# One program order for all engines from a list-scheduled model; transposes of the first two batches on TensorE

## The chip, the cores and the metric

The kernel runs on one core of one Trainium2 chip. The metric is the device time of one execution in microseconds. A profiled execution gives a trace: each engine's instructions with start and length, the DMA queues, and the clock that TensorE was granted. Engines are named as in the profile: PE is TensorE's matmul side, PEld its weight loads, DVE is VectorE, ACT is ScalarE, POOL is GpSimd, SP is SyncE; an added q (SPq) means the engine's queue of instructions that it issues, such as DMAs.

## The reference

For 8 batches, 12 heads, 448 positions and head size 64, q and k are normalized by their root mean square over the head dimension and multiplied by a gain vector each; then softmax attention; then the heads are put side by side (3584 tokens of 768) and go through a feed-forward layer with a gate.

```python
q_n, k_n = rmsnorm(q, g_q), rmsnorm(k, g_k)        # x / sqrt(mean(x*x) + 1e-6) * g
attn = softmax(q_n @ k_n.T / sqrt(64))
x = (attn @ v)  -> (3584, 768)
h = x @ w_in                                       # 768 x 2048
out = (h * sigmoid(1.702 * h)) @ w_out             # 2048 x 768, float32
```

## The kernel before

Work goes by pairs of heads: 48 pairs, numbered i, six to a batch. A sequence of 448 is 4 blocks of 112. Per pair the steps are these.

- `load`: three DMAs from SP bring q, k and v of the pair (112 partitions, 224 KB each), into a ring of 7 pairs.
- `square` (POOL, line 166) and `reduce` (DVE, line 173) give sums of squares. `rsqrt` (DVE, lines 187 to 198) makes the inverse root for a group of pairs: pairs 0, 1 and 2 are groups of one, the others go by threes. It is a bit trick and two Newton steps, 11 small operations on 16 (one pair) or 48 (three pairs) elements.
- `norm` (POOL, line 206, one operation for q and one for k) writes the normalized tile `qkn` in bf16; `vcast` (DVE, line 214) writes v in bf16 to `vx`.
- `dmaT` (line 219): one DMA transpose from SP turns `qkn` to `qT`. `pad` (DVE, line 228) scales k by the gains into `kz`, twice (one half of the partitions each).
- `Sc`: per block of 112 keys two matmuls to a score tile `sc` (PSUM, two buffers), and one `exp` on ACT (line 240) to `att`.
- `PV`: per head 16 matmuls of 65 columns to `o`, then a reciprocal and a multiply on DVE (lines 259, 260) to `obs`.
- `OT` (line 272): one DMA transpose from SP puts the pair's 128 rows into `xT[b]`.

When the six pairs of a batch are in `xT[b]`, its feed-forward can run: 16 tiles `gp` of 6 matmuls (line 299), a tanh on ACT (line 307) and a gate on DVE (line 309) for each, then the second product `op`, 16 matmuls a tile (line 327), a copy on ACT (line 334) and a store from SP. The weights come by DMAs from POOL's queue with a cast to bf16 (lines 378 and 388).

The order of every engine's instructions is the order in which the program emits them. It is written by hand: a loop over pairs emits a block of scores, PV of the pair before at blocks 0 and 2, the steps for later pairs (`ahead`: loads 7 pairs ahead, squares 6, reduces 5, norms 2), and then `fill` puts in feed-forward matmuls worth 1525 ns of a small clock that the emission keeps. That clock delays the emission of evictions, gates, transposes and pads by fixed times (`later`). At the start `start` emits seven pairs of loads (21 DMAs), then the steps of pair 0, the six loads of `w_in`, squares up to pair 5, and the four loads of `w_out`. The program ends with all the feed-forward that is left.

Of the kernel before, what the change touches and what calls it, by code (L numbers as in the profile page):

```python
# [18 lines left out]
_MAGIC = 0x5F3759DF  # L19


@with_exitstack
def kernel(
# [24 lines left out]
    AW = (NS - 1) * SS + WIN  # L48

# [56 lines left out]
    raw = [None] * NG  # L106
    vraw = [None] * NG
    rs = [None] * NG
    qkn = [None] * NG
    qT = [None] * NG  # L110
    obs = [None] * NG
    xT = [None] * B
    groups = [[0], [1], [2], [3, 4, 5]] + [list(range(j, j + 3)) for j in range(6, NG, 3)]
    group_of = {p: g for g in groups for p in g}
    ssq_of = {}

    clk = 0.0
    events = []  # L120
    seq = 0

    done = set()

    def later(dt, f, tag=None):
        nonlocal seq
        seq += 1
        heapq.heappush(events, (clk + dt, seq, f, tag))

    def step():  # L130
        nonlocal clk
        t, _, f, tag = heapq.heappop(events)
        clk = max(clk, t)
        f()
        done.add(tag)

    def tick(dt):
        nonlocal clk
        end = clk + dt
        while events and events[0][0] <= end:  # L140
            step()
        clk = end

    def need(*tags):

        while any(t not in done for t in tags):
            step()

    def load(i):
        b, h0 = i // NP, 2 * (i % NP)  # L150
        t = raw_p.tile([128, 2, 2, NS, D], FP32, tag="raw", name="raw")
        for gi, src in enumerate((q, k)):
            nc.sync.dma_start(  # L153
                out=t[:SS, gi, :, :, :],
                in_=src[b, h0:h0 + 2].rearrange("h (ss ns) d -> ss h ns d", ns=NS))
        tv = vraw_p.tile([128, 2, NS, D], FP32, tag="vraw", name="vraw")
        nc.sync.dma_start(
            out=tv[:SS, :, :, :],
            in_=v[b, h0:h0 + 2].rearrange("h (ss ns) d -> ss h ns d", ns=NS))
        raw[i], vraw[i] = t, tv  # L160

    sq_of = {}

    def square(i):
        sq = sq_p.tile([128, 2, 2, NS, D], FP32, tag="sq", name="sq")
        nc.gpsimd.tensor_tensor(out=sq[:SS], in0=raw[i][:SS], in1=raw[i][:SS], op=ALU.mult)  # L166
        sq_of[i] = sq

    def reduce(i):
        grp = group_of[i]  # L170
        if i == grp[0]:
            ssq_of[grp[0]] = stat_p.tile([128, 3, 2, 2, NS], FP32, tag="ssq", name="ssq")
        nc.vector.reduce_sum(out=ssq_of[grp[0]][:SS, i - grp[0]], in_=sq_of.pop(i)[:SS],  # L173
                             axis=AX.X)

    def rsqrt(i):
        grp = group_of[i]
        if i != grp[-1]:
            return

        m = len(grp) * 4 * NS
        x = ssq_of[grp[0]][:SS].rearrange("p a b c d -> p (a b c d)")[:, :m]
        y = stat_p.tile([128, 3, 2, 2, NS], FP32, tag="rs", name="rs")
        yf = y[:SS].rearrange("p a b c d -> p (a b c d)")[:, :m]
        t = small_p.tile([128, 3 * 4 * NS], FP32, tag="nt", name="nt")
        tf = t[:SS, :m]
        nc.vector.tensor_scalar(out=x, in0=x, scalar1=float(D) * 1e-6, scalar2=None,
                                op0=ALU.add)
        nc.vector.tensor_scalar(out=tf.bitcast(I32), in0=x.bitcast(I32), scalar1=1,  # L189
                                scalar2=None, op0=ALU.arith_shift_right)  # L190
        nc.vector.tensor_tensor(out=yf.bitcast(I32), in0=magic[:SS, :m],
                                in1=tf.bitcast(I32), op=ALU.subtract)
        for _ in range(2):
            nc.vector.tensor_tensor(out=tf, in0=yf, in1=yf, op=ALU.mult)  # L194
            nc.vector.tensor_tensor(out=tf, in0=tf, in1=x, op=ALU.mult)  # L195
            nc.vector.tensor_scalar(out=tf, in0=tf, scalar1=-0.5, scalar2=1.5,  # L196
                                    op0=ALU.mult, op1=ALU.add)
            nc.vector.tensor_tensor(out=yf, in0=yf, in1=tf, op=ALU.mult)  # L198
        for p in grp:
            rs[p] = (y, p - grp[0])  # L200

    def norm(i):
        y, a = rs[i]
        t = qkn_p.tile([128, 2, NS, 2, D], BF16, tag="qkn", name="qkn")
        for gi in range(2):
            nc.gpsimd.tensor_tensor(  # L206
                out=t[:SS, gi],
                in0=raw[i][:SS, gi].rearrange("p h n d -> p n h d"),
                in1=y[:SS, a, gi].rearrange("p h n -> p n h").to_broadcast([SS, NS, 2, D]),
                op=ALU.mult)  # L210
        qkn[i] = t

    def vcast(i):
        nc.vector.tensor_copy(out=vx_ring[i % N_V][:SS, :, :, :D], in_=vraw[i][:SS])  # L214

    def dmaT(i):

        t = qT_p.tile([128, 2, NS * SS], BF16, tag="qT", name="qT")
        nc.sync.dma_start_transpose(
            out=t[:, :, :].rearrange("p g (n s) -> p (g n) s", s=SS),  # L220
            in_=qkn[i][:SS].rearrange("s g n h d -> s (g n h d)"))
        qT[i] = t

    def pad(i):
        kz = kz_ring[i % N_KZ]
        for hp in range(2):
            r = slice(64 * hp, 64 * hp + 64)
            nc.vector.tensor_scalar(out=kz[r, hp, :], in0=qT[i][r, 1, :], scalar1=gG[r, :],  # L228
                                    scalar2=None, op0=ALU.mult)


    def Sc(i, kc):
        need(("T", i))
        sc = ps_sc.tile([128, 2, 512], FP32, tag="sc", name="sc")
        for hp in range(2):
# [3 lines left out]
            tick(190)  # L239
        later(250, lambda: nc.scalar.activation(  # L240
            out=att_ring[i % N_ATT][:SS, kc, :, :S], in_=sc[:SS, :, :S], func=ACT.Exp), ("E", i, kc))

    def PV(i, hp):
        need(*[("E", i, kc) for kc in range(NS)])
        att, vx = att_ring[i % N_ATT], vx_ring[i % N_V]
# [216 lines left out]
```

## Time and profile before

| | |
|---|---|
| median of 3 runs | 529.82 us (528.68 to 531.94) |
| the profiled execution | 535.25 us, of which span 533.5 us |
| mean granted TensorE clock | 0.958 |
| busy: PE, PEld | 441.6 us (83%), 270.6 us (51%) |
| busy: DVE, ACT, POOL | 311.8 (58%), 266.1 (50%), 199.5 us (37%) |

The busy share of TensorE in 40 equal slices of the span (13.3 us each; a digit is tenths), and the granted clock in tenths below it:

```profile
PE   0005175589999799999997999999999999999996
PEclk9999987559999899999998999999999999999999
```

Full clock is 2.4 GHz, the other level is 1.2 GHz. The time of an execution is 1.75 us longer than its span.

### The profile page before, as it was taken

What the parts mean: (1) busy time and instruction counts of PE and PEld (TensorE: products, weight loads), DVE (VectorE), ACT (ScalarE), POOL (GpSimd) and SP (SyncE); (2) the same over time, 40 slices, a digit from 0 to 9 for tenths busy, and PEclk for the clock granted to TensorE, in tenths of its full rate; (3) what the DMA queues carried; (4) which work ended last, traced back from release to release, by engine and by line L of the source; (5) the groups of instructions that cost most, each with busy time, mean ns of one, the idle gap of its engine ahead of it and who ended that gap; (6) DMA issues with size and microseconds to landing.
All of it is one profiled execution on the core that took longest, in us unless ns stands there. A gap on an engine that the chain in (4) does not pass through costs nothing.

```text
span 533.5 us, 9224 instructions
## 1 busy us (share of the span) xinstructions
PE 441.6 (83%) x3584; PEld 270.6 (51%) x3584; DVE 311.8 (58%) x719; ACT 266.1 (50%) x377; POOL 199.5 (37%) x165
## 2 busy tenths in 40 slices
PE   0005175589999799999997999999999999999996
PEld 0002043345665356665664566656665666565553
DVE  3254276766848684669487856487669564621500
ACT  0004053436656464576564655666576556752421
POOL 2773635543435343533526353535253440000000
PEclk9999987559999899999998999999999999999999
DMA  6999946473577535884679347747684433112012
GB/s 152 228 226 181 210 125 151 105 173 80 117 140 163 136 80 149 174 169 89 124 176 186 79 92 185 163 102 124 166 174 113 88 91 74 36 39 76 1 40 80
DMA packets 109964, 67.46 MB, mean 126 GB/s; under 512 B 71264, under 2 KB 105568, under 8 KB 109920
## 3 DMA queue, kind: packets, MB, share of 16 engines
q1 hardware_dynamic: 106944, 60.58, 52.0%
q0 software_dynamic: 2976, 6.29, 6.7%
q8 instruction: 28, 0.46, 0.4%
q14 instruction: 16, 0.13, 0.1%
HBM read 45.61 MB, written 11.01 MB: 106 GB/s over the span
## 4 chain that ended last, share of the span: by engine, by line
PE 62%; DMA 13%; DVE 12%; POOL 4%; SPq 3%; issue 3%; ACT 1%; POOLq 0%; DVEq 0%
PE op L327 25%; PE gp L299 22%; DMA qT<-qkn 9%; PE sc L236 9%; PE o L251 7%; DMA raw<-in_k_dram 4%; POOL sq L166 3%; DVE kz L228 3%; DVE ssq L173 2%; DVE g L309 2%; DVE obs L260 1%; POOL qkn L206 1%; SPq L153 1%; DVE nt L189 1%; DVE nt L195 1%
## 5 line engine op out<-in xcount | busy, mean ns | idle before, releaser
L240 ACT ACTIVATE att<-sc 112x896 bf16<-112x896 f32 x192 | 174.3, 916 | 179.1 <-PE sc L236 178.0
L236 PE MATMUL sc<-qT,kz 128*112 128x448 bf16 x384 | 117.1, 392 | 74.0 <-DVE kz L228 72.2
L299 PE MATMUL gp<-xt,w_in_s 128*128 128x448 bf16 x768 | 164.2, 359 | 10.1 <-DVE g L309 9.2
L166 POOL TENSOR_TENSOR sq<-raw 112x1024 f32<-112x1024 f32 x48 | 92.2, 1922 | 195.0 <-DMA raw<-in_k_dram 77.5
L327 PE MATMUL op<-w_out_s,g 128*128 128x384 bf16 x896 | 159.2, 326 | 0.0
L206 POOL TENSOR_TENSOR qkn<-raw,rs 112x512 bf16<-112x512 f32 x96 | 101.4, 1077 | 45.1 <-DVE rs L198 31.6
L327 PEld LDWEIGHTS <-g 128*128 128x128 bf16 x896 | 85.0, 98 | 54.3
L299 PEld LDWEIGHTS <-w_in_s 128*128 128x128 bf16 x768 | 73.6, 99 | 75.3 <-issue 15.8
L236 PEld LDWEIGHTS <-kz 128*112 128x112 bf16 x384 | 52.2, 141 | 107.2 <-DVE kz L228 82.2
L309 DVE SCALAR_TENSOR_TENSOR g<-th,gp 128x448 bf16<-128x448 f32 x128 | 78.0, 619 | 45.6 <-ACT th L307 44.2
L307 ACT ACTIVATE th<-gp 128x448 f32<-128x448 f32 x128 | 69.4, 542 | 44.9 <-PE gp L299 42.7
L228 DVE TENSOR_SCALAR kz<-qT,gG 64x448 bf16<-64x448 bf16 x96 | 59.0, 615 | 54.3 <-DMA qT<-qkn 53.3
L251 PEld LDWEIGHTS <-att 112*128 112x128 bf16 x1536 | 67.4, 103 | 20.8 <-DVE obs L260 5.6
L251 PE MATMUL o<-vx,att 112*128 112x65 bf16 x1536 | 70.7, 201 | 2.9 <-DVE obs L260 2.8
L173 DVE TENSOR_REDUCE ssq<-sq 112x16 f32<-112x1024 f32 x48 | 58.0, 1210 | 13.3 <-POOL sq L166 13.2
L259 DVE RECIPROCAL rcp<-o 112x4 f32<-112x4 f32 x96 | 17.3, 180 | 68.8 <-PE o L251 68.5
L334 ACT ACTIVATE osb<-op 128x384 f32<-128x384 f32 x56 | 27.4, 489 | 38.3 <-PE op L327 36.9
L260 DVE TENSOR_TENSOR obs<-o,rcp 112x256 bf16<-112x256 f32 x96 | 40.8, 425 | 3.3
L214 DVE CAST vx<-vraw 112x512 bf16<-112x512 f32 x48 | 22.8, 475 | 0.0
L194 DVE TENSOR_TENSOR nt<-rs 112x48 f32<-112x48 f32 (+1 forms) x36 | 9.0, 249 | 1.2
L195 DVE TENSOR_TENSOR nt<-nt,ssq 112x48 f32<-112x48 f32 (+1 forms) x36 | 8.9, 246 | 1.2
L196 DVE TENSOR_SCALAR nt<-nt 112x48 f32<-112x48 f32 (+1 forms) x36 | 8.3, 230 | 1.2
(18 smaller groups left out, 35.3 us busy)
## 6 DMA issues: line engine op xcount, KB each, us to landing
raw<-in_q_dram SPq DMA_DIRECT2D x48, 224.0 KB, 3.3
raw<-in_k_dram SPq DMA_DIRECT2D x48, 224.0 KB, 3.6
vraw<-in_v_dram SPq DMA_DIRECT2D x48, 224.0 KB, 4.0
w_in_s<-in_moe_w_in_dram POOLq DMA_DIRECT2D x6, 512.0 KB, 15.5
w_out_s<-in_moe_w_out_dram POOLq DMA_DIRECT2D x4, 768.0 KB, 20.5
out_dram<-osb SPq DMA_DIRECT2D x8, 336.0 KB, 3.2
out_dram<-osb SPq DMA_DIRECT2D x8, 288.0 KB, 3.0
out_dram<-osb SPq DMA_DIRECT2D x8, 240.0 KB, 3.0
```

What stands on the lines that cost most here:

```text
L166: nc.gpsimd.tensor_tensor(out=sq[:SS], in0=raw[i][:SS], in1=raw[i][:SS], op=ALU.mult)
L173: nc.vector.reduce_sum(out=ssq_of[grp[0]][:SS, i - grp[0]], in_=sq_of.pop(i)[:SS], axis=AX.X)
L206: nc.gpsimd.tensor_tensor(out=t[:SS, gi], in0=raw[i][:SS, gi].rearrange("p h n d -> p n h d"), in1=y[:SS, a, gi].rearrange("p h n -> p n h ...
L228: nc.vector.tensor_scalar(out=kz[r, hp, :], in0=qT[i][r, 1, :], scalar1=gG[r, :], scalar2=None, op0=ALU.mult)
L236: nc.tensor.matmul(sc[:SS, hp, :S], lhsT=kz_ring[i % N_KZ][:, hp, kc * SS:(kc + 1) * SS], rhs=qT[i][:, 0, :], start=True, stop=True)
L240: later(250, lambda: nc.scalar.activation(out=att_ring[i % N_ATT][:SS, kc, :, :S], in_=sc[:SS, :, :S], func=ACT.Exp), ("E", i, kc))
L251: nc.tensor.matmul(o[:, qs, :], lhsT=att[:SS, kc, hp, qs * SS:qs * SS + WIN], rhs=vx[:SS, hp, kc, :], start=(kc == 0), stop=(kc == NS - 1))
L260: nc.vector.tensor_tensor(out=obs[i][:SS, :, hp, :], in0=o[:SS, :, :D], in1=rcp[:SS, :].to_broadcast([SS, NS, D]), op=ALU.mult)
L299: nc.tensor.matmul(ps[:, :], lhsT=w_in_s[:, ki, m * 128:(m + 1) * 128], rhs=xT[b][:, ki, :], start=(ki == 0), stop=(ki == KI - 1))
L307: later(250, lambda: nc.scalar.activation(out=th[:, :], in_=ps[:, :], func=ACT.Tanh, scale=0.851))
L309: later(1000, lambda: nc.vector.scalar_tensor_tensor(out=g_of[b // 2][:, m, lo:lo + S], in0=th[:, :], scalar=1.0, in1=ps[:, :], op0=ALU.ad ...
L327: nc.tensor.matmul(ps[:, :], lhsT=g_of[b // 2][:, ko, tm * 128:(tm + 1) * 128], rhs=w_out_s[:, ko, half * HALF:(half + 1) * HALF], start=( ...
```

## The change

The hand-written emission goes away. Each instruction, or a few of one engine, is a task with an engine, an assumed duration in ns, a latency, a priority key, predecessors, and at times a slot of a ring that it takes. A list scheduler (`_Order.run`) plays the engines against a clock: an engine that is free takes the ready task with the lowest key, and the task's instructions are emitted at that moment. So the program order on each engine is the order of the model; on the chip the engines run it in order. The keys are in units of pairs: scores of pair i at i + block/4, feed-forward at 7.3 plus the work already listed over 5800 ns, steps that prepare pair i at i minus 1 to i minus 3.

What the instructions are changes too:

- squares run on ACT, in two halves for pairs 0 and 1;
- of the inverse root DVE keeps two operations (`seed`), and POOL does the other nine (`rsqrt`);
- `vcast` is on POOL, as a multiply by a column of ones;
- for pairs 0 to 11 `qkn` and `obs` are turned by TensorE (8 and 4 transposes of 112 x 128) into a PSUM buffer of the ring of three that the feed-forward uses, and DVE copies them out (`take_q`, `take_k`, `take_x`); the other 36 pairs keep the two DMA transposes;
- `pad` walks its elements in another order (112 groups of 4, step 112);
- `w_in` is loaded in four parts of 512 columns in place of six of 128 rows, from 13 us on by the model's clock, 6.5 us apart; `w_out` from 42 us on, 7 us apart;
- the four small loads of the gains and the load of pair 0's k are issued by ACT.

```diff
-    def square(i):
-        nc.gpsimd.tensor_tensor(out=sq[:SS], in0=raw[i][:SS], in1=raw[i][:SS], op=ALU.mult)
+    def square(i, part):
...
+        nc.scalar.activation(out=sq_of[i][:SS, part], in_=raw[i][:SS, part], func=ACT.Square)
...
+    def rsqrt(grp):
...
+        nc.gpsimd.tensor_tensor(out=yf.bitcast(I32), in0=magic[:SS, :m], in1=t.bitcast(I32),
+                                op=ALU.subtract)
         for _ in range(2):
-            nc.vector.tensor_tensor(out=tf, in0=yf, in1=yf, op=ALU.mult)
...
+            nc.gpsimd.tensor_tensor(out=t, in0=yf, in1=yf, op=ALU.mult)
...
     def vcast(i):
-        nc.vector.tensor_copy(out=vx_ring[i % N_V][:SS, :, :, :D], in_=vraw[i][:SS])
+        nc.gpsimd.tensor_tensor(out=vx[:, :, :D], in0=vr,
+                                in1=ones[:SS, :].to_broadcast([SS, 2 * NS, D]), op=ALU.mult)
+    def turn_pe(i):
+        tps[i] = ps_w.tile([128, 2, NS, SS], BF16, tag="w", name="t_ps")
...
+                nc.tensor.transpose(tps[i][:, gi, s, :], qkn[i][:SS, gi, s, :, :],
+                                    ident[:SS, :SS])
+    def take_q(i):
...
+        nc.vector.tensor_copy(out=qT[i][:, 0, :],
+                              in_=tps[i][:, 0].rearrange("p n s -> p (n s)"))
+    def take_k(i, hp):
+        nc.vector.tensor_scalar(out=kz_ring[i % N_KZ][r, hp, :],
+                                in0=tps[i][:, 1].rearrange("p n s -> p (n s)")[r],
+                                scalar1=gG[r, :], scalar2=None, op0=ALU.mult)
+    def pad(i, hp):
+            out=kz_ring[i % N_KZ][r, hp, :].rearrange("p (n s) -> p s n", s=SS),
+            in0=qT[i][r, 1, :].rearrange("p (n s) -> p s n", s=SS),
...
+        for j, part in enumerate(parts):
+            od.add(("S", i, j), "ACT", 920 / len(parts) + 80,
+                   lambda i=i, p=part: square(i, p), i - 3,
...
+            od.add(("Q", i), "POOL", 2300 if len(group_of[i]) > 1 else 1700,
+                   lambda g=group_of[i]: rsqrt(g), i - 2.6, deps=[("Q0", i)])
+        for gi in range(2):
+            od.add(("N", i, gi), "POOL", 1080, lambda i=i, gi=gi: norm(i, gi), i - 2.4,
+                   deps=[("Q", group_of[i][-1]), ("T", i - N_QKN)])
+        od.add(("V", i), "POOL", 1000, lambda i=i: vcast(i), i - 1.6,
+               deps=[("L", i, 2), ("P", i - N_V, 1, NS - 1)])
+        if i < ON_PE:
+            od.add(("T", i), "PE", 400, lambda i=i: turn_pe(i), i - 1.0,
...
+        else:
+            od.add(("T", i), "SP", 400, lambda i=i: turn_dma(i), i - 10.0,
...
+        for kc in range(NS):
+            od.add(("C", i, kc), "PE", 380, lambda i=i, kc=kc: score(i, kc), i + kc / 4,
+                   deps=[("K", i, 0), ("K", i, 1), ("KQ", i)], lat=250,
+                   takes=("sc", ("E", i, kc)))
+            od.add(("E", i, kc), "ACT", 917, lambda i=i, kc=kc: expo(i, kc), i + kc / 4 - 1,
+                   deps=[("C", i, kc), ("P", i - N_ATT, 1, NS - 1)])
...
+    for c in range(4):
+        od.add(("WI", c), "POOL", 800, lambda c=c: load_in(c), -50, at=13000.0 + 6500.0 * c,
...
+        od.add(("WO", c), "POOL", 800, lambda c=c: load_out(c), -50, at=42000.0 + 7000.0 * c,
...
+    PACE = 5800.0
+    for b in range(B):
+        for m in range(MI):
+            key = 7.3 + done / PACE
+            od.add(("F", b, m), "PE", KI * 189, lambda b=b, m=m: first(b, m), key,
+                   deps=[("X", b * NP + p) for p in range(NP)] + [("WI", m // 4), last],
+                   lat=250, takes=("w", ("G", b, m)))
+            done += KI * 189
...
+    od.run()
```

## Rows read from the trace of the kernel before

**Rows 1.** The page's first part: busy us (share of span) x instructions.

```profile
span 533.5 us, 9224 instructions
PE 441.6 (83%) x3584; PEld 270.6 (51%) x3584; DVE 311.8 (58%) x719; ACT 266.1 (50%) x377; POOL 199.5 (37%) x165
```

**Rows 2.** Windows: stretch, length, busy us (x count) per engine, clock, DMA, GB/s.

```profile
0.00:42.50 42.50, 0.00 (x0) 0.00 (x0) 17.11 (x51) 1.28 (x1) 24.87 (x33) 1.00 0.99 199
42.50:116.20 73.70, 40.78 (x306) 23.81 (x307) 42.94 (x94) 29.02 (x33) 34.02 (x26) 0.77 0.77 154
116.20:490.40 374.20, 362.63 (x3065) 225.50 (x3062) 241.79 (x559) 223.15 (x320) 140.58 (x107) 0.99 0.56 122
490.40:533.50 43.10, 38.17 (x219) 21.33 (x218) 9.94 (x16) 12.61 (x24) 0.00 (x0) 0.99 0.16 46
```

**Rows 3.** Waits up to 116.2: who, for whom, us, times, longest.

```profile
PE sc L236 <- DVE kz L228: 72.2, 15, 42.5
DVE kz L228 <- DMA qT<-qkn: 24.0, 6, 10.4
```

**Rows 4.** Timeline of the start: start us, us, engine, line, operation.

```profile
7.72 1.89 POOL L166 TENSOR_TENSOR sq<-raw 112x1024 f32<-112x1024 f32 x1 [6.35 <-DMA raw<-in_k_dram]
13.24 2.19 POOL L206 TENSOR_TENSOR qkn<-raw,rs 112x512 bf16<-112x512 f32 x2 [3.63 <-DVE rs L198]
15.37 3.40 POOL L378 DMA_DIRECT2D w_in_s<-in_moe_w_in_dram  x6
20.45 19.82 SPq L219 DMA_TRANSPOSE qT<-qkn  x2
```

**Rows 5.** Tile qT: the transposes' time from issue to landing.

```profile
DMA to landing us min/median/max: 2.9/4.1/21.6
```

**Rows 6.** Chain of waits at the start: start us, us, what.

```profile
3.92 3.65 DMA raw<-in_k_dram
```

**Rows 7.** Timeline around the first feed-forward matmul.

```profile
116.23 2.06 PE L299 MATMUL gp<-xt,w_in_s 128*128 128x448 bf16 x5
```

**Rows 8.** Groups by line and shape: count | busy us, mean ns | idle before.

```profile
L240 ACT ACTIVATE att<-sc 112x896 bf16<-112x896 f32 x192 | 174.3, 916 | 179.1 <-PE sc L236 178.0 <-ACT th L307 0.2
L307 ACT ACTIVATE th<-gp 128x448 f32<-128x448 f32 x128 | 69.4, 542 | 44.9 <-PE gp L299 42.7 <-DVE nt L189 0.7 <-DVE nt L196 0.6
L206 POOL TENSOR_TENSOR qkn<-raw,rs 112x512 bf16<-112x512 f32 x96 | 101.4, 1077 | 45.1 <-DVE rs L198 31.6 <-issue 13.5
L166 POOL TENSOR_TENSOR sq<-raw 112x1024 f32<-112x1024 f32 x48 | 92.2, 1922 | 195.0 <-DMA raw<-in_k_dram 77.5 <-DVE ssq L173 58.0 <-DVE vx L214 18.9
L214 DVE CAST vx<-vraw 112x512 bf16<-112x512 f32 x48 | 22.8, 475 | 0.0
L194 DVE TENSOR_TENSOR nt<-rs 112x16 f32<-112x16 f32 x6 | 1.0, 174 | 0.2
L173 DVE TENSOR_REDUCE ssq<-sq 112x16 f32<-112x1024 f32 x48 | 58.0, 1210 | 13.3 <-POOL sq L166 13.2
L309 DVE SCALAR_TENSOR_TENSOR g<-th,gp 128x448 bf16<-128x448 f32 x128 | 78.0, 619 | 45.6 <-ACT th L307 44.2
L260 DVE TENSOR_TENSOR obs<-o,rcp 112x256 bf16<-112x256 f32 x96 | 40.8, 425 | 3.3
L299 PE MATMUL gp<-xt,w_in_s 128*128 128x448 bf16 x768 | 164.2, 359 | 10.1 <-DVE g L309 9.2 <-DMA xt<-obs 0.7
L251 PE MATMUL o<-vx,att 112*128 112x65 bf16 x1536 | 70.7, 201 | 2.9 <-DVE obs L260 2.8
L240 ACT ACT_TABLE_LOAD x1 | 1.3, 1283 | 0.7 <-PEq L446 0.7
```

**Rows 9.** Tile kz: the pads' shortest, median and longest ns.

```profile
L228 DVE TENSOR_SCALAR kz<-qT,gG x96: 320/339/1962, 41.6 to 463.6; 64x448 bf16<-64x448 bf16 x96
```

**Rows 10.** The page's sixth part: weight loads, KB each, us from issue to landing.

```profile
w_in_s<-in_moe_w_in_dram POOLq DMA_DIRECT2D x6, 512.0 KB, 15.5
w_out_s<-in_moe_w_out_dram POOLq DMA_DIRECT2D x4, 768.0 KB, 20.5
```

More of the change, by code (lines that the diff above doesn't have):

```diff
@@ L137, in tick @@
[L137 to L149, printed above, removed]
-        b, h0 = i // NP, 2 * (i % NP)
[L151 to L160, printed above, removed]
@@ L199, in rsqrt, with norm @@
         for p in grp:
             rs[p] = (y, p - grp[0])
[L202 removed]
+    def norm(i, gi):
         y, a = rs[i]
[L204 to L211 removed]
@@ L238, in Sc, with expo @@
                              rhs=qT[i][:, 0, :], start=True, stop=True)
[L239 to L245, printed above, removed]
+    def expo(i, kc):
+        nc.scalar.activation(out=att_ring[i % N_ATT][:SS, kc, :, :S],
+                             in_=scs.pop((i, kc))[:SS, :, :S], func=ACT.Exp)
@@ new lines, with first, tanh @@
+    g_of, gps, ops = {}, {}, {}
+    def first(b, m):
+        ps = gps[b, m] = ps_w.tile([128, S], FP32, tag="w", name="gp")
+        for ki in range(KI):
+            nc.tensor.matmul(ps[:, :], lhsT=w_in_s[:, ki, m * 128:(m + 1) * 128],
+                             rhs=xT[b][:, ki, :], start=(ki == 0), stop=(ki == KI - 1))
+    ths = {}
+    def tanh(b, m):
+        th = ths[b, m] = th_p.tile([128, S], FP32, tag="th", name="th")
+        nc.scalar.activation(out=th[:, :], in_=gps[b, m][:, :], func=ACT.Tanh, scale=0.851)
@@ new lines, in gate, with second @@
+    def gate(b, m):
+        if m == 0 and b % 2 == 0:
+            g_of[b // 2] = g_p.tile([128, MI, 2 * S], BF16, tag="g", name="g")
+        lo = (b % 2) * S
+        nc.vector.scalar_tensor_tensor(
+            out=g_of[b // 2][:, m, lo:lo + S], in0=ths.pop((b, m))[:, :], scalar=1.0,
+            in1=gps.pop((b, m))[:, :], op0=ALU.add, op1=ALU.mult)
+    def second(bp, tm, hf, c):
+        if c == 0:
+            ops[bp, tm, hf] = ps_w.tile([128, HALF], FP32, tag="w", name="op")
+        for ko in range(4 * c, 4 * c + 4):
+            nc.tensor.matmul(ops[bp, tm, hf][:, :],
+                             lhsT=g_of[bp][:, ko, tm * 128:(tm + 1) * 128],
+                             rhs=w_out_s[:, ko, hf * HALF:(hf + 1) * HALF],
+                             start=(ko == 0), stop=(ko == MI - 1))
@@ L393, in ahead @@
-    def ahead(i, s):
-        if s == 0:
-            if i + LOAD < NG:
-                load(i + LOAD)
-            if i + SQ < NG:
-                square(i + SQ)
-        if s == 1 and i + RED < NG:
-            reduce(i + RED)
-        if s == 2 and i + RED < NG:
-            rsqrt(i + RED)
-        if s == 1 and i + NORM < NG:
-            prepare(i + NORM)
-    def prepare(j):
-        norm(j)
-        vcast(j)
-        later(2600, lambda: dmaT(j))
-        later(6000, lambda: pad(j), ("T", j))
@@ L413 @@
-    start()
-    tick(2000)
-    for i in range(NG + 1):
-        for s in range(NS):
-            if i < NG:
-                Sc(i, s)
-            if s == 0 and i > 0:
-                PV(i - 1, 0)
-            if s == 2 and i > 0:
-                PV(i - 1, 1)
-            ahead(i, s)
-            fill(per_gap)
-        if i > 0:
-            OT(i - 1)
-    while ready < B - 1:
-        step()
-    fill(1e12)
-    tick(1e9)
-    assert pos == len(moe)
+    PACE = 5800.0
+    done = 0.0
+    last = None
```

480 lines of the change are left out of this document (295 added, 185 removed).

## The prediction

> **What bounds the kernel now.** I read the page's busy shares first [rows 1]: TensorE is busy 441.6 of 533.5 us, the others half the span. So either TensorE's own work is the bound or its idle time is. The windows by stage answer that [rows 2]. Up to 42.5 us TensorE does nothing. From 42.5 to 116.2 us it is busy 40.78 of 73.70 us at a mean granted clock of 0.77, that is, partly at the lower of the two levels. From 116.2 us to the end it is busy 362.63 + 38.17 = 400.8 of 417.3 us at 0.99. At 116.23 us the first feed-forward matmul starts [rows 7]; it needs the rows of all six pairs of batch 0. So the kernel has two parts: a start of 116 us in which TensorE has only attention to do and waits 42.5 + 32.9 = 75.4 us, and 417 us in which it is the bound and waits 16.5 us. A faster engine helps the second part little; what the change can win lies in the first.
>
> Who ends the waits there [rows 3]: of TensorE's waits, 72.2 us end with the pad of k, and 24.0 us of the pad's own with the transposing DMA. The timeline shows how [rows 4]: the first pair's q and k are normalized at 13.24 + 2.19 = 15.43 us, but SyncE comes to their transpose at 20.45 us, behind 21 loads, and is held 19.82 us by the first two, among loads, weights and transposes that all use the DMA engines at a share near 1 [rows 2]. A transpose lands 4.1 us after its issue in the median and 21.6 us at worst [rows 5]. Squares of 1.92 us and norms of 2 x 1.08 us a pair [rows 8] stand in line on GpSimd besides, with the issue of the weight loads (3.40 us) between [rows 4].
>
> **The start after the change, in steps.** Data of pair 0: k was issued at 3.92 us behind four small loads and landed 3.65 us later, at 7.57 us [rows 6]. It now stands behind the same four on ScalarE's queue; I leave 7.57. Square of half a pair on ScalarE: the exp of 896 elements takes 916 ns and the tanh of 448 takes 542 [rows 8], so 0.835 ns an element and 168 ns fixed; 512 elements 0.60 us, 1024 elements 1.02 us. Half a reduce: 1.21/2 + 0.05 = 0.66 us. Two seed operations: 2 x 0.174 = 0.35 us.
>
> Newton on GpSimd is not in the trace. Its two-input operations there cost 1922 ns for 1024 elements and 1077 for 512, so 1.65 ns an element and some 0.23 us fixed: I take 0.25 us for 16 elements and 0.30 for 48, nine of them 2.25 and 2.7 us. Lower end: VectorE's 0.174 us; upper end: 0.5 us, half a norm. The value cast I take at a norm's 1.08 us, as it has the same shape and two inputs. The rows speak against moving these: the cast took 0.475 us on VectorE [rows 8]. The Trainium skill (GPSIMD Engine Reference, Engine selection) says likewise that elementwise work with two inputs runs about twice as slow there as on VectorE. By that factor alone, an estimate, a Newton operation would be 0.35 us, and the time below would come out some 3 us longer.
>
> So norms of pair 0 end at 7.57 + 0.60 + 0.66 + 0.35 + 2.25 + 2.15 = 13.6 us. From there GpSimd sets the pace, with 0.57 us for each weight part that it issues (3.40/6): cast and issue 1.65, Newton and norms 4.4 for pair 1: 19.7; the same for pair 2: 25.7; cast and issue: 27.4; Newton for the group 3 to 5: 30.1; three pairs of norms, two casts, one issue 9.2: 39.3 us. Then pair 5: eight transposes on TensorE, 1.0 us (bounds for one: 46 ns, as an o matmul in the stream, and 0.2 us, its length alone [rows 8]); three evictions by VectorE from PSUM, 0.6 us each (the gate's 619 ns for the same 448 elements is the nearest): 42.1; four exps and one square that gets between: 4 x 0.916 + 1.02 = 4.7: 46.8; last PV and its division 1.7: 48.5; four transposes and a copy 1.2: 49.7 us.
>
> TensorE may bind instead. At full clock a pair costs 8 x 0.214 + 70.7/48 = 3.2 us [rows 8], at half clock 6.4. Scores of pair 0 can start at 13.6 + 2.8 = 16.4 us; six pairs at half clock and the last steps of 1.8 us give 56.6 us. I take 52 us for the first feed-forward matmul, nearer the GpSimd end, since the clock was 0.77 in the stretch of this kind [rows 2]. VectorE has 1.3 + 0.35 + 1.8 + 2 x 0.6 + 0.6 = 5.3 us a pair, under GpSimd's 6.1. Low end 46 (Newton at 0.174, full clock), high end 60 (Newton at 0.5 us adds 36 x 0.23 = 8 us).
>
> **The rest.** 417.3 us stays [rows 2]. At 116.2 us TensorE had done 306 matmuls, 7.65 pairs of 40; at 52 us it will have done 6, so 1.65 x 3.2 = 5.3 us are still to do. The transposes of pairs 6 to 11 are 72 more, 3.3 to 14 us by the bounds above; I take 5.
>
> The other engines have room where TensorE goes by pairs: 40.35 pairs in 374.2 us, 9.3 us each. ScalarE then has 4 x 0.916 + 1.02 + 2.67 x 0.542 + 0.6 = 6.7 us; VectorE loses the cast and nine small operations; GpSimd changes squares (1.92) for cast and Newton (1.08 + 0.9). The pads have cost 320 ns free and up to 1962 [rows 9], the long ones beside a square of GpSimd; with another walk I give them 0.3 to 1.1 us and nothing on the path, because a pair's transposes may start as soon as the scores three pairs earlier are done, some 18 us ahead, against 4.1 us to land. If that cover goes, the price is a stall of TensorE per pair.
>
> The idle time of the second part, 16.5 us, I leave: a new fixed order may remove what waits for the gate (9.2 us, [rows 8]) and may add as much. Sum of the span: 52 + 417.3 + 5.3 + 5 = 479.6 us, and 1.75 us around it, 481.4 us against the profiled 535.25. The median of the runs is 0.990 of the profiled time (529.82/535.25), so **477 us**.
>
> **Rivals.** A: *the frozen order gives part of it back.* Engines run in order what a model with fixed durations has listed, and TensorE's place for a score group is where the model frees one of two score buffers. If score groups and gates come late by 0.1 to 0.15 us on average, some 300 places cost 30 to 45 us: 507 to 520 us. For it: no slack in the model at these places. Against it: the assumed durations (380 ns for two scores, 917 an exp, 1080 a norm) are those of the rows.
>
> B, the other side: *ScalarE's queue holds each score buffer.* Behind each of 168 score groups after 52 us stands not only an exp but a square (1.02 us) or a tanh (0.54) that the order puts first. The gain of 53 us is gone from 53/168 = 0.31 us a group, and from 0.35 us it is slower by over 1%; at 0.5 us the time is 477 + 84 = 561 us. Against it: ScalarE's 6.7 of 9.3 us.
>
> C: *squares change ScalarE's tables.* The trace has a single table load, of 1.283 us, for exp, tanh and copy [rows 8]; a square has not been there. If square lay in another table, 50 squares would bring 100 loads: 6 x 2.6 = 15 us in the start, and ScalarE at 6.7 + 2.6 = 9.3 us a pair, level with TensorE: 492 to 500 us. The Trainium skill (ScalarE: Activation LUTs, Table sets) says that functions in one set need no reload and does not list square beside exp and tanh, though it has cheap functions in every set. By its 2.66 us a switch, an estimate, ScalarE would have 12 us a pair and the time would be near 600 us.
>
> D: *the weights come late.* The first quarter of w_in must land by 52 us, issued near 14; loads of a sixth took 15.5 us and quarters of w_out 20.5 [rows 10]. If the start moves too little for that, 485 to 500 us. That nothing is gained at all would need the first transposes on TensorE to wait for something as late as 42.5 us; nothing in the start does.
>
> **How the numbers follow.** My sum has 0.72, A 0.13, B 0.06, C 0.03, D 0.04, no gain 0.02. The range: low, start 46, transposes 3.3 and 12 us less idle time: 457; A reaches 520, of which I take the lower half: 512. What is outside: upper A, B, the far ends. A change within 1% (5.3 us) could not be told from none. Faster by over 1%: 0.91; same 0.02; slower 0.07 (B, and C at its dear end).
>
> **What would show it.** In the changed kernel's trace: scores of pair 0 at 16 to 18 us; the first feed-forward matmul at 46 to 60 us; no transposing DMA before pair 12; one table load; nine GpSimd operations of 0.2 to 0.35 us per group; idle time of TensorE after the start of 5 to 30 us. I am wrong if the start is over 65 us, or if TensorE waits more than 40 us later on, on ScalarE's exps above all.

## The result and the profile after

The changed kernel takes 489.96 us (median of four runs, 487.94 to 491.38), the one before 530.07 (528.68 to 531.94): a ratio of 0.924 [0.920, 0.928]. The forecast was 477 in a range of 457 to 512. Faster was right, by the mechanism named; the size is 13 us short. A whole run can come out slower for the same kernel, and the ratios here leave out runs that lie over 1.5% above the fastest of their kernel.

The changed kernel's page, its first part and two slice rows, answers to [rows 1]:

```profile
span 488.3 us, 9605 instructions
PE 440.4 (90%) x3728; PEld 271.5 (56%) x3728; DVE 324.2 (66%) x536; ACT 305.1 (62%) x427; POOL 236.5 (48%) x327
...
PE   0667999987998898999989999989999999999995
...
PEclk9986999999999799999999999999999999999999
```

TensorE is busy for 440.4 us where it was 441.6. The work is the same but for 144 transposes; what went is time in which it stood. The windows say where. They answer to [rows 2] and are cut at the first scores, at the first feed-forward matmul and where GpSimd has ended:

```profile
0.00:16.67 16.67, 1.11 (x8) 0.63 (x8) 6.94 (x22) 5.69 (x7) 7.35 (x31) 1.00 0.91 210
16.67:58.95 42.28, 32.70 (x356) 21.93 (x357) 32.11 (x70) 31.07 (x36) 38.16 (x62) 0.88 1.16 246
58.95:434.00 375.05, 357.61 (x3081) 221.18 (x3080) 275.24 (x429) 253.58 (x357) 191.02 (x235) 0.99 0.52 124
434.00:488.30 54.30, 49.00 (x286) 27.75 (x284) 9.93 (x16) 14.74 (x29) 0.00 (x0) 0.99 0.19 54
```

The start went from 116.23 to 58.95 us, 57.3 less. The rest went from 417.3 to 429.35 us, 12.05 more: TensorE is busy there for 357.61 + 49.00 = 406.6 us (400.8 before) and stands 22.7 (16.5 before).

The timeline of the changed kernel at four places of the start answers to [rows 4, 7]: the first of the nine Newton operations of pair 0, its norms, its first scores, and the first feed-forward matmul. The columns are those of [rows 4], with the idle time of the engine before the group and its releaser in brackets:

```profile
10.49 0.21 POOL L276 TENSOR_TENSOR rs<-magic,seed 112x16 int32<-112x16 int32 x1 [4.47 <-DVE seed L268]
...
13.16 2.07 POOL L291 TENSOR_TENSOR qkn<-raw,rs 112x512 bf16<-112x512 f32 x2
...
16.67 0.62 PE L343 MATMUL sc<-qT,kz 128*112 128x448 bf16 x1 [0.83 <-DVE kz L319]
...
58.95 1.30 PE L485 MATMUL gp<-xt,w_in_s 128*128 128x448 bf16 x6
```

The first scores stand 1.4 us behind the end of the norms, where before the two transposing DMAs alone were held 19.82 us [rows 4]. TensorE's waits up to 58.95 us, in the columns of [rows 3], have changed their names with it:

```profile
PE t_ps L309 <- POOL qkn L291: 18.6, 11, 14.3
PE sc L343 <- ACT att L348: 2.1, 6, 0.7
PE sc L343 <- DVE kz L319: 0.8, 1, 0.8
```

The 72.2 us behind the pad of k [rows 3] are 0.8, behind its copy out of PSUM, and 14.3 of the 18.6 us behind GpSimd's norms are the time until the first transpose. After the start TensorE waits for this (same view, 58 to 488 us):

```profile
PE o L355 <- DVE obs L366: 6.8, 4, 3.1
PE gp L485 <- DVE g L500: 2.9, 6, 0.9
PE o L355 <- POOL vx L300: 2.7, 3, 1.8
PE o L355 <- ACT att L348: 1.9, 2, 1.8
```

The groups by line and shape, in the columns of [rows 8]:

```profile
L291 POOL TENSOR_TENSOR qkn<-raw,rs 112x512 bf16<-112x512 f32 x96 | 123.8, 1311 | 80.9 <-DMA qT<-qkn 80.2
L300 POOL TENSOR_TENSOR vx<-vraw,ones 112x512 bf16<-112x512 f32 x48 | 60.8, 1268 | 41.4 <-PE o L355 30.7 <-issue 7.4 <-DMA vraw<-in_v_dram 3.1
L247 ACT ACTIVATE sq<-raw 112x1024 f32<-112x1024 f32 x46 | 48.4, 1057 | 21.4 <-DMA raw<-in_k_dram 18.7 <-DVE ssq L266 1.6 <-ACT sq L247 0.5
L247 ACT ACT_TABLE_LOAD x1 | 1.3, 1283 | 3.9 <-issue 3.9
```

Rows of the tiles kz, qkn and qT, with min/median/max in ns and then the first and last start, answer to [rows 5, 9]:

```profile
L333 DVE TENSOR_SCALAR kz<-qT,gG x72: 1224/1406/2151, 90.0 to 407.0; 64x448 bf16<-64x448 bf16 x72
...
L291 POOL TENSOR_TENSOR qkn<-raw,rs x96: 1047/1058/2013, 13.2 to 380.6; 112x512 bf16<-112x512 f32 x96
...
DMA to landing us min/median/max: 2.9/3.1/5.6
```

One row was not foreseen. The pad of k, 320 ns free and 339 in the median [rows 9], takes 1224 ns at best; 72 of them are 113.9 us of VectorE. Norms, at most 1241 ns before, reach 2013. This stretch of the timeline shows how it comes to TensorE:

```profile
156.35 1.06 POOL L291 TENSOR_TENSOR qkn<-raw,rs 112x512 bf16<-112x512 f32 x1
156.43 3.85 DVE L333 TENSOR_SCALAR kz<-qT,gG 64x448 bf16<-64x448 bf16 x2
...
157.36 1.89 POOL L300 TENSOR_TENSOR vx<-vraw,ones 112x512 bf16<-112x512 f32 x1
...
160.31 0.18 DVE L365 RECIPROCAL rcp<-o 112x4 f32<-112x4 f32 x1
160.53 0.42 DVE L366 TENSOR_TENSOR obs<-o,rcp 112x256 bf16<-112x256 f32 x1
...
161.10 0.60 PE L355 MATMUL o<-vx,att 112*128 112x65 bf16 x8 [3.15 <-DVE obs L366]
```

Two pads hold VectorE for 3.85 us. The division that frees `o` stands behind them in VectorE's queue, and TensorE's next PV needs `o`: it waits 3.15 us. Beside the pads a cast takes 1.89 us. Behind this wait TensorE is slower for some us, as eight matmuls of one kind show right behind it and 8 us later:

```profile
162.51 2.75 PE L508 MATMUL op<-w_out_s,g 128*128 128x384 bf16 x8
...
171.00 1.46 PE L508 MATMUL op<-w_out_s,g 128*128 128x384 bf16 x8
```

From 160 to 170 us the mean granted clock is 0.66, so for part of it the lower level. With contiguous pads (below) TensorE has no such wait there and a granted clock of 1.00 in the same 10 us.

### The profile page after: what moved, and what is told of

It is laid out like the page before. It is cut to its first block, busy times and chain, and to the rows that moved or that the text cites. A ratio compares the mean times of both kernels' runs of the same rounds, so it can differ in the third digit from the quotient of the medians.

```text
span 488.3 us, 9605 instructions
## 1 busy us (share of the span) xinstructions
PE 440.4 (90%) x3728; PEld 271.5 (56%) x3728; DVE 324.2 (66%) x536; ACT 305.1 (62%) x427; POOL 236.5 (48%) x327
## 4 chain that ended last, share of the span: by engine, by line
PE 45%; DVE 19%; POOL 14%; DMA 12%; issue 4%; ACT 3%; SPq 1%; ACTq 0%; POOLq 0%; DVEq 0%
PE op L508 19%; PE gp L485 15%; DVE kz L333 9%; POOL qkn L291 7%; PE sc L343 6%; DMA qT<-qkn 5%; PE o L355 5%; DVE ssq L253 4%; DMA raw<-in_k_dram 4%; DVE g L500 3%; DMA raw<-in_q_dram 2%; ACT sq L247 2%; POOL vx L300 2%; DVE obs L366 2%; POOL rs L283 1%
## 5 line engine op out<-in xcount | busy, mean ns | idle before, releaser
L508 PE MATMUL op<-w_out_s,g 128*128 128x384 bf16 x896 | 169.3, 328 | 0.1
L291 POOL TENSOR_TENSOR qkn<-raw,rs 112x512 bf16<-112x512 f32 x96 | 123.8, 1311 | 80.9 <-DMA qT<-qkn 80.2
L333 DVE TENSOR_SCALAR kz<-qT,gG 64x448 bf16<-64x448 bf16 x72 | 113.9, 1582 | 9.1 <-DMA qT<-qkn 8.3
L355 PEld LDWEIGHTS <-att 112*128 112x128 bf16 x1536 | 82.3, 99 | 57.2 <-issue 12.8
L343 PE MATMUL sc<-qT,kz 128*112 128x448 bf16 x384 | 108.2, 369 | 3.0 <-ACT att L348 2.1
L355 PE MATMUL o<-vx,att 112*128 112x65 bf16 x1536 | 92.8, 196 | 15.8 <-DVE obs L366 7.5
L300 POOL TENSOR_TENSOR vx<-vraw,ones 112x512 bf16<-112x512 f32 x48 | 60.8, 1268 | 41.4 <-PE o L355 30.7
L253 DVE TENSOR_REDUCE ssq<-sq 112x16 f32<-112x1024 f32 (+1 forms) x50 | 58.4, 1172 | 21.3 <-ACT sq L247 17.9
L247 ACT ACTIVATE sq<-raw 112x1024 f32<-112x1024 f32 (+1 forms) x50 | 50.7, 1022 | 24.1 <-DMA raw<-in_k_dram 21.4
L365 DVE RECIPROCAL rcp<-o 112x4 f32<-112x4 f32 x96 | 17.6, 184 | 59.2 <-PE o L355 58.4
L309 PE MATMUL t_ps<-ident,qkn 112*128 112x112 bf16 x96 | 10.0, 247 | 18.8 <-POOL qkn L291 18.6
L309 PEld LDWEIGHTS <-qkn 112*128 112x128 bf16 x96 | 6.9, 113 | 22.6 <-POOL qkn L291 21.4
## 6 DMA issues: line engine op xcount, KB each, us to landing
w_in_s<-in_moe_w_in_dram POOLq DMA_DIRECT2D x4, 768.0 KB, 12.6
```

The costliest lines, as they stand in the source:

```text
L247: nc.scalar.activation(out=sq_of[i][:SS, part], in_=raw[i][:SS, part], func=ACT.Square)
L253: nc.vector.reduce_sum(out=ssq_of[g0][:SS, i - g0, part], in_=sq_of[i][:SS, part], axis=AX.X)
L291: nc.gpsimd.tensor_tensor(out=qkn[i][:SS, gi], in0=raw[i][:SS, gi].rearrange("p h n d -> p n h d"), in1=y[:SS, a, gi].rearrange("p h n -> ...
L300: nc.gpsimd.tensor_tensor(out=vx[:, :, :D], in0=vr, in1=ones[:SS, :].to_broadcast([SS, 2 * NS, D]), op=ALU.mult)
L333: nc.vector.tensor_scalar(out=kz_ring[i % N_KZ][r, hp, :].rearrange("p (n s) -> p s n", s=SS), in0=qT[i][r, 1, :].rearrange("p (n s) -> p ...
L343: nc.tensor.matmul(sc[:SS, hp, :S], lhsT=kz_ring[i % N_KZ][:, hp, kc * SS:(kc + 1) * SS], rhs=qT[i][:, 0, :], start=True, stop=True)
```

## The experiments

The theory: the start was won by transposes that TensorE makes at once, with an order and a split of work that feed it, and the pads' walk took part of it back. A turn is a transpose of `qkn` or `obs`, the split is which engine has which operation, the walk is the order in which a pad goes through its elements. The rivals: the order alone or the split alone is the gain; the walk costs nothing. All medians are of four runs. The kernel before, run beside them, came out at 528.86 to 530.98, so two kernels that were not run side by side can seem up to 2 us apart without being so; the ratio is to the kernel before that ran beside it. "First F" is the first feed-forward matmul of the profiled run.

| kernel | us | ratio [95%] | first F, us |
|---|---|---|---|
| changed kernel | 489.96 | 0.924 [0.920, 0.928] | 58.95 |
| contiguous pads | 469.89 | 0.889 [0.885, 0.893] | 59.6 |
| changed, all turns by DMA | 541.42 to 563.07 | - | 133.9 |
| hand order, TensorE turns | 514.11 | 0.973 [0.969, 0.978] | 100.2 |
| changed, groups of one | 498.15 | 0.943 [0.938, 0.949] | 63.2 |
| contiguous, squares on GpSimd | 491.28 | 0.925 [0.923, 0.927] | 67.5 |
| contiguous, Newton on VectorE | 474.03 | 0.893 [0.890, 0.895] | 58.4 |
| contiguous, casts on VectorE | 477.63 | 0.900 [0.898, 0.902] | 61.8 |
| contiguous, VectorE kept busy | 485.64 | 0.915 [0.911, 0.918] | 59.7 |
| contiguous, old split | 511.39 | 0.963 [0.957, 0.969] | 84.5 |
| contiguous, all turns by DMA | 508.62 | 0.955 [0.948, 0.962] | 102.4 |
| contiguous, six pairs turned | 478.65 | 0.902 [0.895, 0.909] | 56.7 |
| contiguous, pair 3 alone | 469.16 | 0.885 [0.878, 0.893] | 58.1 |

**Contiguous pads.** The changed kernel with its pad walking as before; the order of all engines stays.

```diff
-            out=kz_ring[i % N_KZ][r, hp, :].rearrange("p (n s) -> p s n", s=SS),
-            in0=qT[i][r, 1, :].rearrange("p (n s) -> p s n", s=SS),
+            out=kz_ring[i % N_KZ][r, hp, :],
+            in0=qT[i][r, 1, :],
```

> The changed kernel with the pads' walk alone undone (one run of 448 in place of 112 groups of 4); program order untouched. Theory (the new walk costs VectorE and GpSimd, and TensorE's later waits come from there): a pad falls from 1406 ns in the median to about 340, norms on GpSimd from a mean of 1311 to about 1080 ns, the 10.8 us that TensorE waits for divisions and casts after the start shrink by more than half, time 480 to 486 us. Rival (pads are off the path): pads as short, time within 2 us of 490. Second rival (the contiguous pad blocks GpSimd more): 492 us or more.

Measured: 469.89 us, 20.1 less, at least twice what the theory had (4 to 10). Its tile of pads:

```profile
L333 DVE TENSOR_SCALAR kz<-qT,gG x72: 318/446/1229, 90.7 to 385.7; 64x448 bf16<-64x448 bf16 x72
```

Its windows, cut at its first F:

```profile
0.00:59.60 59.60, 34.17 (x364) 22.46 (x365) 39.01 (x91) 36.63 (x43) 45.52 (x92) 0.94 1.07 240
59.60:467.90 408.30, 400.74 (x3366) 248.64 (x3363) 221.54 (x446) 268.77 (x385) 153.82 (x235) 1.00 0.50 120
```

TensorE's waits from there on, the two longest:

```profile
PE o L355 <- ACT att L348: 1.5, 2, 0.8
PE o L355 <- DVE obs L366: 0.4, 1, 0.4
```

The rest of the kernel goes from 429.35 to 408.3 us. TensorE stands 7.6 us there, not 22.7, and for as many matmuls (3366, 3367) is busy 400.7 us, not 406.6, at a granted clock of 1.00, not 0.99: 15.1 + 5.9 us. The 6.8 us of waits for the division are 0.4. In this order the walk cost some 20 us, where VectorE had 67 us more of pads (113.9 against 46.6). The order was listed with 540 ns for a pad, though, and an order listed with the 1.2 us and more that this walk takes was not run: it might put the divisions ahead.

**VectorE kept busy.** Is it VectorE's own time, or GpSimd, which the pads also hold? Here each contiguous pad is followed by a reduce that nobody reads and that touches no tile of the others.

```diff
+        nc.vector.reduce_sum(out=fsum[:SS], in_=filler[:SS], axis=AX.X)
```

> Contiguous pads, and behind each pad of pairs 12 to 47 one more VectorE operation that nothing reads: a sum of 112 x 832 numbers, about 1.0 us, in VectorE's own time and on no port of GpSimd's. It gives back the VectorE time that the changed pads took, without their holding GpSimd. Theory (the 20 us came from VectorE's time: divisions and gates late in its queue): 483 to 492 us. Rival (they came from holding GpSimd, whose norms took 1.31 in place of 1.07 us): under 475 us with norms at 1.07 us.

Measured: 485.64 us. The filler's tile:

```profile
L340 DVE TENSOR_REDUCE fsum<-filler x72: 1002/1014/1023, 91.1 to 404.7; 112x13 f32<-112x832 f32 x72
```

GpSimd's norms, by line and shape:

```profile
L294 POOL TENSOR_TENSOR qkn<-raw,rs 112x512 bf16<-112x512 f32 x96 | 100.6, 1071 | 90.5 <-DMA qT<-qkn 89.8 <-POOL qkn L294 0.2
```

TensorE's longest wait after its start:

```profile
PE o L359 <- DVE obs L370: 8.6, 8, 2.2
```

The theory held. The norms are free (1071 ns) and GpSimd's busy time is that of contiguous pads, while pads and filler together take 114.3 us of VectorE, as the changed kernel's pads did (113.9). That alone takes 15.75 of the 20.07 us back, with the same wait for the division on top. The other 4.3 us fit the 34 us by which pads make norms and casts longer; no run here shows them by themselves, and the two ratios nearly touch.

**Who wins the start: turns, order, split.** One kernel has the turns alone, two take the split or the turns away from the full version. A hand order with the new split was not run. First the hand-written order of before with its own split, and only the transposes of pairs 0 to 11 moved to TensorE:

```diff
+        if j < ON_PE:
+            later(2600, lambda: turn_pe(j), ("T", j))
+            return
```

> The kernel before, its hand-written order and its split of the engines, with one part of the change alone: pairs 0 to 11 are turned by TensorE and copied out by VectorE. Theory (transposes): the first feed-forward matmul moves from 116 us to 65 to 85 us, time 485 to 505 us, so at least two thirds of the gain. Rival (order and engine split): first feed-forward matmul later than 95 us, time over 510 us.

Measured: 514.11 us, first F at 100.2: the theory's 65 to 85 us fell, and the rival held. TensorE's two longest waits up to there:

```profile
PE o L254 <- DVE obs L263: 23.0, 12, 5.2
PE sc L239 <- DVE kz L425: 20.9, 1, 20.9
```

The DMA's part is gone, yet the copy of pair 0's k out of PSUM kept TensorE waiting for 20.9 us: by hand it stands on VectorE behind reduces of pairs 1 to 4, which wait for GpSimd's squares. The turn is ready and the queue isn't. Another place for that copy in the hand order was not tried, so the 514.11 us are those of this placing.

Next the new order and TensorE's turns with contiguous pads, but the old split: squares back on GpSimd, Newton and casts on VectorE, listed with their durations there.

```diff
-        nc.scalar.activation(out=sq_of[i][:SS, part], in_=raw[i][:SS, part], func=ACT.Square)
+        nc.gpsimd.tensor_tensor(out=sq_of[i][:SS, part], in0=raw[i][:SS, part],
+                                in1=raw[i][:SS, part], op=ALU.mult)
...
-                                in1=ones[:SS, :].to_broadcast([SS, 2 * NS, D]), op=ALU.mult)
+        nc.vector.tensor_copy(out=vx[:, :, :D], in_=vr)
...
-            od.add(("Q", i), "POOL", 2300 if len(group_of[i]) > 1 else 1700,
+            od.add(("Q", i), "DVE", 2200 if len(group_of[i]) > 1 else 1700,
```

> The scheduled order and TensorE's transposes with the old split of the engines: squares on GpSimd, Newton and casts on VectorE, contiguous pads. Beside the hand order with TensorE's transposes (514.1 us, also old split) it gives what the scheduled order is worth alone; beside 469.9 us what the new split is worth. Theory (the order gives most of the rest, the split some 20 us, nearly all of it the squares): 485 to 497 us, first feed-forward matmul at 64 to 72 us. Rival (the order needs the split): 505 us or more.

Measured: 511.39 us, first F at 84.5: 2.7 us better than by hand, and by the ratios some 5. The casts, by line and shape:

```profile
L301 DVE CAST vx<-vraw 112x512 bf16<-112x512 f32 x48 | 49.5, 1032 | 0.1
```

TensorE's longest wait up to 84.5 us that is VectorE's:

```profile
PE sc L343 <- DVE kz L319: 10.3, 3, 5.4
```

The mean of a cast, 475 ns [rows 8], is 1032 here, and 642 in the run below that moves the casts alone. The median is 423 ns, as before (420). What lifts the mean are a few casts that stand as long as GpSimd goes from one operation to the next, as here:

```profile
48.73 7.40 DVE L301 CAST vx<-vraw 112x512 bf16<-112x512 f32 x1
48.89 5.11 POOL L292 TENSOR_TENSOR qkn<-raw,rs 112x512 bf16<-112x512 f32 x5
53.97 1.88 POOL L247 TENSOR_TENSOR sq<-raw 112x1024 f32<-112x1024 f32 x1
```

The cast ends at 56.13 us, 0.3 us behind GpSimd's square. Two more in the start, of 3.94 and 6.07 us, end just so, 0.3 us behind an unbroken run of GpSimd's. VectorE, busy 354.5 us, is late in the start. The rival held: the order is worth little without the split.

Last the turns. With contiguous pads, order and split stay and all 48 pairs are turned by DMA:

```diff
-    ON_PE = NP * 2
+    ON_PE = 0
```

> The scheduled order and the new split with DMA transposes for all pairs and contiguous pads. Theory (without TensorE's transposes the start is lost, whatever the order, because transposes stand among loads and weights on SyncE's queue): first feed-forward matmul at 105 us or later, time 510 to 535 us. Rival (the loss of the earlier run of this kind came from its long pads): first feed-forward matmul before 90 us, time under 500 us.

Measured: 508.62 us, first F at 102.4, both just under the theory's figures and far from the rival's. TensorE's longest wait up to there:

```profile
PE sc L343 <- DVE kz L333: 41.0, 9, 26.2
```

The tile qT, its DMAs' time to landing in us:

```profile
DMA to landing us min/median/max: 2.9/3.3/18.9
```

The same edit on the changed kernel:

> The changed kernel with the DMA transposes for all 48 pairs; the list scheduler gives the order again. Theory (the start is won by taking the transposes off the DMA queues): the first feed-forward matmul moves from 59 us to 75 us or later, time 505 to 540 us. Rival (the scheduled order and the freed GpSimd win the start, whoever transposes): the first feed-forward matmul before 68 us, time under 500 us.

It ran in 541.42 to 563.07 us, a spread so wide that no ratio is formed. The theory's 505 to 540 us were too short, and all four runs are slower than any of the kernel before beside them (524.87 to 531.93). Its first F, at 133.9 in the run of 563.07, stands on the same side. Why it loses so much more than with contiguous pads was not tried apart.

From 469.89 us, then, the loss is 38.7 us without TensorE's turns and 41.5 without the split; turns alone give 14.7 (528.86 - 514.11). The parts don't add: each takes away the wait that is longest once the others are there. No run takes the order away alone, so what it is worth beside the turns and the new split stays open.

**Which part of the split.** One moved operation at a time is put back on its old engine, with contiguous pads (edits as in the old split's).

> The changed kernel with contiguous pads (469.9 us) and squares back on GpSimd, scheduled there at 1.9 us each. Theory (GpSimd's work per pair paces the start): 6 to 8 squares more on GpSimd before the first feed-forward matmul, which moves from 59.6 us to 70 to 76 us; time 480 to 487 us. Rival (the start is paced by something else: loads, ScalarE, TensorE at half clock): first feed-forward matmul before 63 us, time under 474 us.

> Contiguous pads and the nine Newton operations back on VectorE, scheduled there at 2.2 us. Theory (GpSimd paces the start): five Newton runs of 1.9 to 2.6 us leave GpSimd in the start, first feed-forward matmul at 50 to 55 us, time 460 to 466 us. Rival (VectorE, with evictions, reduces and Newton, becomes the pace; or the place doesn't matter): first feed-forward matmul at 58 us or later, time 468 us or more.

> Contiguous pads and the value casts back on VectorE as copies, scheduled there at 0.48 us. Theory (GpSimd paces the start): six to eight casts of 1.04 us leave GpSimd in the start, first feed-forward matmul at 52 to 56 us, time 462 to 467 us. Rival (casts wait for GpSimd's operations on the shared port, as in the kernel before, where one took up to 2.1 us): casts of 0.7 us and more in the mean, time 469 us or more.

Measured: squares on GpSimd 491.28 us (21.4 more, 8 of it in the start), Newton on VectorE 474.03 (4.1 more), casts on VectorE 477.63 (7.7 more). For casts the rival held: they win on GpSimd although a cast is slower there (1043 ns against a median of 422). Newton came out at the rival's time, but its interval meets that of contiguous pads (0.890 to 0.895 against 0.885 to 0.893): that it is worth its place on GpSimd is not shown, only that taking it off wins nothing. For squares the direction held, while the first F came earlier (67.5) and the time later than the theory had them. Put back alone, the squares cost half of what the whole split does: 46 whole ones take 48.4 us of ScalarE in the changed kernel and 87.2 of GpSimd here.

**Six pairs turned.** With contiguous pads and `ON_PE = NP`, pairs 6 to 11 go by DMA.

> Contiguous pads, TensorE's transposes for pairs 0 to 5 only. Theory (the start needs them for batch 0; in batch 1 TensorE is the bound and 72 transposes cost it 3 to 5 us): 465 to 468 us. Rival (after pair 5 the DMA queues still hold weights and loads, so scores of pairs 6 to 8 come late): 471 us or more with waits of TensorE for pads.

Measured: 478.65 us, 8.8 more, though F starts 2.9 us earlier. The rival's time held: while the loads run, a transposing DMA still takes up to 15.3 us to land, and the second batch is better off with TensorE's turns. The rival's waits for pads come to 2.7 us after the first F; TensorE also waits 4.6 us for exps there, and how the 8.8 us divide is not shown.

**Groups of the start.** Pairs 3, 4 and 5 share one inverse root, and pair 3's norms wait for pair 5's squares. First the changed kernel with six groups of one, then contiguous pads with pair 3 alone and the pad's assumed time cut to 450 ns.

```diff
-    groups = [[0], [1], [2], [3, 4, 5]] + [list(range(j, j + 3)) for j in range(6, NG, 3)]
+    groups = [[j] for j in range(6)] + [list(range(j, j + 3)) for j in range(6, NG, 3)]
```

```diff
-    groups = [[0], [1], [2], [3, 4, 5]] + [list(range(j, j + 3)) for j in range(6, NG, 3)]
+    groups = [[0], [1], [2], [3], [4, 5]] + [list(range(j, j + 3)) for j in range(6, NG, 3)]
```

> The changed kernel with pairs 3, 4 and 5 as groups of one for the inverse root (two more sets of nine small GpSimd operations). Theory (pair 3 waits in the start for the reduces of pairs 4 and 5, so ScalarE and TensorE stand still from 35 to 41 us): scores of pair 3 start at 30 to 34 us in place of 40.5, first feed-forward matmul 53 to 57 us in place of 59, time 484 to 488 us. Rival (GpSimd's total work sets the pace of the start): first feed-forward matmul at 59 us or later, time 490 us or more.

> Contiguous pads, planned at 450 ns as measured; pair 3 alone and pairs 4 and 5 together for the inverse root, in place of one group of three. Theory (the group hands ScalarE the exps of three pairs at once, so it stands still before and is the pace afterwards; one Newton run more costs GpSimd 2.6 us): scores of pair 3 before 38 us, first feed-forward matmul 55 to 58 us, 464 to 468 us. Rival (GpSimd's added work costs as much): first feed-forward matmul at 59 us or later, 469 us or more.

Measured: six groups of one 498.15 us, 8.2 more, first F at 63.2; pair 3's scores start at 35.87 us, 4.6 earlier, but GpSimd ends pair 5's norms at 46.66, 3.7 us later, with two Newton runs more. That speaks for GpSimd's total as the pace (the rival). Pair 3 alone: 469.16 us against 469.89, no difference that these runs can tell; F is 1.5 us earlier. With F at 58.1 us the result lies between the theory's figures and the rival's. These two kernels, at ratios of 0.885 and 0.889, are the best here and beat both the kernel before and the changed one.

## Why the prediction was right, and where not

**The start: the mechanism held, the size was 7 us short.** First scores were put at 16 to 18 us and came at 16.67; the first F at 52 (46 to 60) and came at 58.95. The first of these has luck in it: pair 0's norms ended at 13.16 + 2.07 = 15.23 us and not at 13.6, as the square of its k began at 8.52 us and not at 7.57 and its nine Newton operations took 2.67 us and not 2.25; from there to the scores it took 1.4 us and not 2.8. GpSimd was to end pair 5's norms at 39.3 us and ended at 42.99: 1.6 us are that late start, 1.4 the four weight issues (0.88 to 1.02 us each, not 0.57), and 1.1 the other three Newton runs, less 0.4 that norms, casts and idle time give back. Then "four exps and one square" were counted for pair 5. The group of three gives its pairs to ScalarE at once. ScalarE's groups in the changed kernel's timeline:

```profile
34.35 1.08 ACT L247 ACTIVATE sq<-raw 112x1024 f32<-112x1024 f32 x1
41.45 1.72 ACT L348 ACTIVATE att<-sc 112x896 bf16<-112x896 f32 x2 [6.03 <-PE sc L343]
...
51.76 3.37 ACT L348 ACTIVATE att<-sc 112x896 bf16<-112x896 f32 x4
```

The windows from 41.45 us on, and of the 6.03 us ahead:

```profile
41.45:57.00 15.55, 13.23 (x166) 9.33 (x165) 13.50 (x30) 14.40 (x17) 14.77 (x23) 0.92 1.16 247
35.42:41.45 6.03, 4.17 (x38) 2.96 (x36) 5.43 (x10) 0.01 (x1) 5.98 (x7) 0.50 1.18 251
```

ScalarE stands for 6.03 us and is then busy for 14.40 of 15.55: twelve exps of pairs 3 to 5 and two squares, 13 us where 4.7 were counted. But four engines are nearly full in that stretch, and with pair 3 alone F came only 1.5 us earlier. That no single term would have given the 52 is argued from this, not shown.

**The operations that moved.** The forecast took 0.25 to 0.30 us for a Newton operation, 1.08 for a cast and 1.02 for a square. Measured: 0.20 to 0.22 us on 16 elements, 0.23 to 0.35 on 48, 1.04 for the free cast, 1.06 for the square. The Newton operations start further apart than they are long, though: nine on 16 elements take from 10.49 to 13.16 us, 0.30 us each, so the term of 2.25 us was short by 0.4. The rows against moving them and the Trainium skill (GPSIMD Engine Reference, Engine selection), which has such work about twice as slow there, are borne out by the cast, 1043 ns against 475; the Newton operations, 0.20 to 0.35 us against VectorE's 0.17 to 0.32, lose less than that. Neither decides. The casts, put back, make the kernel slower, and Newton does not make it faster; the long casts above are one way in which VectorE loses by it, and how much of the 7.7 us they are was not tried apart.

**The pads: this step failed.** The prediction gave them "0.3 to 1.1 us and nothing on the path, because a pair's transposes may start" some 18 us ahead. They took 1.22 to 2.15 us and cost 20. The cover named was that of the transposes, and it held: they land 5.6 us after their issue at the latest. What it left out is the engine's own queue: divisions, for which TensorE waits, stand behind the pads. The price of the walk was not in the trace of before, and the bound of 1.1 us was too low. A row of after has it: 1224 ns at best, against 318 with contiguous pads. The model had planned it with 540 ns. The Trainium skill (SBUF — State Buffer, Specifications (TRN2)) says that SBUF has lines of 16 bytes and that an access which crosses to a new line pays. The pad's inner step is 112 elements of 2 bytes, so each access crosses; the trace agrees, with the price that the page doesn't give. Whether all of that price is the lines', no run here shows. The same page (Who interferes with whom) lists `tensor_scalar` among VectorE's operations that can lock GpSimd out for a whole instruction. The norms of up to 2013 ns beside the pads agree; by the filler run this is the smaller part, the 4.3 us that it left.

**The rest: 429.35 us where 427.6 were forecast,** close, but by luck, out of two misses. With contiguous pads it is 408.3, so the pads' 21 us hid that the rest was estimated 19.3 us too long. Of these, 8.9 are idle time (7.6, not 16.5: half of it is gone) and 10.4 busy time. By first F TensorE has done 364 matmuls, scores and transposes of later pairs among them, where some 312 were assumed; that these 52 are most of the 10.4 us is not shown. The "72 transposes, 5 us" were bounded well: a row of four takes 0.36 us at full clock and 0.56 at half, so 18 rows at full clock are 6.5 us.

**The factor of 0.990** between profiled run and median was wrong for this kernel: profiled run 490.08, median 489.96. It is worth 4.3 us. So 477 + 7.0 (start) + 1.7 (rest) + 4.3 (factor) = 490.0.

**The rivals.** A (a frozen order that gives back 30 to 45 us) was not it: 22.7 us of idle time after the start are in its direction, but 15.1 of them go with the pads, with the order unchanged. B (ScalarE holds the score buffers): waits for exps after the start come to 1.9 us. C (table loads): one load of 1283 ns in the run. D (weights late): no wait of TensorE on a weight load; a quarter of `w_in` landed in 12.6 us [rows 10]. "No gain" would have needed a late first transpose; it stands at 14.27 us.

## What to carry to other kernels

Cover must be named for the queue, not for the data: a step with 18 us to spare still costs time when a short operation that the bound engine needs stands behind it on the same engine. Look up the access pattern of each operation that a change touches; an inner step that leaves the line made one of 0.32 us one of 1.22. Parts of a schedule are worth what the others let through (14.7 us for the turns alone, 38.7 with order and split), so take parts away from the full version as well as adding them to the old one. A mean can hide two kinds of operation: casts of 0.42 us and a few of up to 7.4 made a mean of 1.03.

## What was not expected of the hardware

A VectorE operation of 64 x 448 bf16 with an inner step of 224 bytes took 1224 ns at best, contiguous 318. Beside an unbroken run of GpSimd operations a VectorE cast of 0.42 us took up to 7.40, until that run was over; in the changed kernel a seed operation of 0.19 us took 2.51 so, and ended at 43.05 us, with pair 5's norms (42.99). GpSimd's small operations cost little: 0.20 to 0.22 us for 16 elements, one every 0.30, against 0.17 on VectorE, one every 0.21. A DMA issue on GpSimd for a weight part held it for 0.88 to 1.02 us in the start, where six in a row took 3.40 [rows 4].
